# A transformer block on one core: the last unit in two tiles of 128 tokens, denominators from four key tiles, Q blocks moved

## The chip, the core and the metric

The kernel runs on one core of one Trainium2 chip. Five engines work side by side: TensorE (PE; its weight loads are shown as PEld) multiplies matrices, VectorE (DVE) and ScalarE (ACT) do elementwise work, GpSimd (POOL) small work, SyncE (SP) issues the transfers. SBUF is the memory that the engines work on, PSUM (8 banks of 128 x 512 fp32) takes the matmuls' results. The metric is device time in microseconds (us) of one launch.

## The reference

One pre-norm transformer block over 2048 tokens of width 1024, all bf16: LayerNorm, attention of 32 heads of 32, output projection and residual; LayerNorm, a feed-forward net of width 3584 with GELU (tanh form), residual.

```python
x = A_x
h = x + _A_ref(_layernorm(x, axis=-1), A_wqkv, A_wo)      # qkv, softmax(q k^T / sqrt(32)) v, wo
h2 = h + _B_ref(_layernorm(h, axis=-1), B_w1, B_b1, B_w2, B_b2)   # gelu(x w1 + b1) w2 + b2
```

The attention weights are 32 x 2048 x 2048 exponentials, and there is a plain softmax over the whole row, with no maximum taken off in the kernel.

## The kernel before

**Tiles.** Heads go in 8 groups `g` of four (4 x 32 = 128 partitions), queries in 8 blocks `qb` (also called units `u`) of 256 tokens. A *job* is one group and one query block. It has 8 *rounds*, each over 256 keys (two key tiles of 128): scores for four heads in one go (`Att.qk`, L756: 8 matmuls of 32 x 128, each head in its own quarter of the rows of the array, 256 queries as columns), two exponentials of 128 x 1024 on ScalarE into `PT` (L779), and P times V (`Job.pv`, L798: 8 matmuls, each head in its own quarter of the columns). The denominators are matmuls with a 32-column block of ones (`Job.den`, L828). To halve their number VectorE first adds the two key tiles of a round into `PS` (L820, three buffers), so a denominator of a round is four matmuls; the last round of a job goes straight from `PT` and takes eight. `Job.finish` (L842) transposes and inverts the denominators and writes the output of the job, transposed, to `OT`, which holds three query blocks (`u = qb % 3`).

**Background.** All that isn't attention (projections, Wo, LayerNorm, FFN) is cut into pieces that fill one of PSUM's banks 6 and 7 (`slot()`); a running job holds one of them for its output and denominators, banks 0 to 5 hold scores. `late_q` (L676) makes Q for a block of 512 tokens from a copy of the normalised x that was stored to DRAM (`x_scratch`), with the weights loaded again; `proj` (L635) makes it from SBUF, where `xnT` and the weights `Wall` lie until the FFN's buffers (`hch`, `gT`, the weight rings of `Rings`) are put over them. Either way Q goes to DRAM (`q_scratch`) and comes back a job at a time (`load_q`, L669). `wo` (L886) makes Wo and the residual of a unit into `hch`, `ln2` (L914) the LayerNorm and its transposes into `hnT`, `ffn1` (L925) the first FFN matrix in 14 blocks of 256 columns with bias on VectorE (L943) and a GELU of five VectorE operations and one tanh (`gelu`, L956), `ffn2` (L969) the second in two halves of 512 columns. W1 and Wo come through a ring of 4 blocks, W2 through one of 7.

**The end.** Unit 7 is worked when attention is over: `wo(7, True)` into banks 0 to 3 with the residual added by a matmul with the identity and drained by ScalarE, then `ffn1(7, True)` with ScalarE's own GELU from PSUM (L952), then both halves of `ffn2`. Its W1 goes into SBUF where K and V lay (`b_w1r`), its FFN1 output over `PT` (`gT7`).

**Order.** The code lists tasks with the buffers they read and write. `Graph.schedule` (L109) then simulates the engines with a cost for each task (`occ`), a latency behind it (`lat`) and 0.1 us for each change of array shape on TensorE, and so fixes one order for each engine, the DMA queue on SP too. `pick_pe` (L1144) chooses for TensorE: scores first, then the closing denominator of a job, P times V when enough rounds wait, else background in the order of listing. `merge_tiles` turns longer stretches of background from four 32-column matmuls into whole ones. On the chip each engine works its list in order and waits on semaphores. The listing from the first FFN unit on is (L1098 to L1123):

```python
    late_q(1, 1, [g for g in range(2, G) if g not in EXTRA])
    wo(0)
    ln2(0)
    late_q(2, 0, range(G))
    late_q(3, 1, range(G))
    ffn1(0)
    ...
    for u in range(6):
        wo(u + 1); ffn2(u, 0); ln2(u + 1); ffn2(u, 1); ffn1(u + 1)
        if u < 5:
            attention(u + 3, range(G))
```

(The loop's five calls stand on lines of their own in the file.) Attention thus runs two units and more ahead of the FFN, and the FFN of a unit can't begin before all eight jobs of that unit are finished.

Of the kernel before, what the change touches and what calls it, by code (L numbers as in the profile page):

```python
# [12 lines left out]
P = 128  # L13
# [47 lines left out]
class Graph:  # L61
# [47 lines left out]
    def schedule(self, pick_pe, pool, switch=0.1, dma_rate=280.0, dma_lat=2.1, dma_issue=0.06):  # L109
# [219 lines left out]
def build_kernel(nc, A_x, A_wqkv, A_wo, B_w1, B_b1, B_w2, B_b2, out):  # L329
# [22 lines left out]
    class Area:  # L352
        def __init__(self, start):
            self.cur = start
# [54 lines left out]
    B_OT = [B_OT_[G * i:G * i + G] for i in range(3)]  # L409
    xrb, B_xrb = sb(ot_lo, "xrb", [P, 8, D], BF, 8)  # L410
# [7 lines left out]
    xnT, B_xnTt = sb(ph0, "xnT", [P, 4, DC, 512], BF, 4, 4)  # L418
    k_hi = Area(B_KT[8 * (G - 2)].lo)
    Wall, B_W = [], []  # L420
    for k in range(6):
        h, b = sb(k_hi if k == 2 else ph0, "Wall%d" % k, [P, DC, 512], BF, 1, 4)
        Wall.append(h)
        B_W.append(b)
# [20 lines left out]
    gT7, B_gT7 = sb(Area(pt_lo), "gT7", [P, FC, 256], BF, FC // 2)  # L445
    gs, B_gs = [gT] * 7 + [gT7], [B_gT] * 7 + [B_gT7]
# [22 lines left out]
    att_area = Area(att_lo)  # L469
    w2_area = Area(att_lo)  # L470
    R2 = Rings((att_area, 14), (w2_area, 7), att_area, 2, "b_")
    assert att_area.cur <= att_hi
# [15 lines left out]
    def c_dve_ps(n):  # L488
        return (120 + n) / 960.0 + 0.02

    def c_dve(n, x=1):
        return (62 + n / x) / 960.0 + 0.085

    def c_act(n, ap_bias=False):
        return 0.073 + (0.093 if ap_bias else 0.0) + n / 1200.0

    def pe(fns, occ, reads=(), writes=(), kind="bg", mode="full", prio=0, after=()):
        return gr.add(E.PE, fns, occ, 0.16, reads, writes, prio, kind, mode, after)
# [45 lines left out]
    def act(fn, n, reads=(), writes=(), prio=0, ap_bias=False, kind="", after=()):  # L544
        return gr.add(E.Activation, fn, c_act(n, ap_bias), 0.14, reads, writes, prio, kind, after=after)

    def dve(fn, occ, reads=(), writes=(), prio=0):
        return gr.add(E.DVE, fn, occ, 0.08, reads, writes, prio)
# [25 lines left out]
    def layer_norm(tiles, prio, norm="dve", stats=None):  # L574
# [6 lines left out]
        for k, (x_ap, B_x, o_ap, B_o) in enumerate(tiles):  # L581
            for c in range(2):
                dve(lambda v, c=c, k=k, x_ap=x_ap: v.bn_stats(st_l[:, i + k, 6 * c:6 * c + 6], x_ap[:, 512 * c:512 * c + 512]),
                    0.68, reads=B_x if isinstance(B_x, list) else [B_x], writes=[B_stl[i + k]], prio=(prio or 1) if stats is None else stats)
# [11 lines left out]
        for k, (x_ap, B_x, o_ap, B_o) in enumerate(tiles):  # L596
            eng, cost = (dve, 0.58) if norm == "dve" else (pool, 3.8)
# [4 lines left out]
    def transposes(src_ap, B_src, bank, dst_ap, B_dst, evac, prio):  # L602
# [9 lines left out]
        else:  # L612
            t = dve(lambda v: v.tensor_copy(dst_ap, src()), 0.70, reads=[bb(bank)], writes=[B_dst])
# [17 lines left out]
    def tr_tile(tt, bank, evac, prio=0):  # L631
        tc, t4 = divmod(tt, 4)
        transposes(xb[:, tt % NXB, :], B_xb[tt % NXB], bank, xnT[:, tc, :, t4 * P:(t4 + 1) * P], B_xnTt[tc][t4], evac, prio)

    def proj(which, g, tc, bank, evac, direct=False):  # L635

        blk, c = divmod(which * D + g * P, 512)
        for dc in range(DC):
            mm(bank, Wall[blk][:, dc, c:c + P], xnT[:, tc, dc, :], dc == 0, dc == DC - 1,
# [55 lines left out]
    def proj_v(tt, q, bank, evac, after=()):  # L695
# [3 lines left out]
        for k in range(2):  # L699
            tc, t4 = divmod(tt + k, 4)  # L700
            for dc in range(DC):
                mm(bank, xnT[:, tc, dc, t4 * P:(t4 + 1) * P], Wall[blk][:, dc, c:c + 256], dc == 0, dc == DC - 1,
# [7 lines left out]
    def proj_v1(tt, g, n, bank, evac, c0=0):  # L710

        for k in range(n):
            tc, t4 = divmod(tt + k, 4)
            for dc in range(DC):
                mm(bank, xnT[:, tc, dc, t4 * P:(t4 + 1) * P], Wall[4][:, dc, P * g:P * g + P], dc == 0, dc == DC - 1,
# [12 lines left out]
    def proj_half(which, hc, bank, evac):  # L728
# [3 lines left out]
        for dc in range(DC):  # L732
            mm(bank, Wall[blk][:, dc, 0:P], xnT[:, tc, dc, 256 * h:256 * h + 256], dc == 0, dc == DC - 1,
# [13 lines left out]
    class Att:  # L747
# [8 lines left out]
        def qk(self, job, r):  # L756


            qb, g = job
            qs = q_slots[qb, g]  # L760
            us = [self.unit % self.n_units, (self.unit + 1) % self.n_units]
            self.unit += 2
            fns, banks = [], []
            for i in range(2):
                for h in range(4):
                    k0 = (2 * r + i) * P

                    def fn(p, i=i, h=h, k0=k0):
                        return p.matmul(psum[:, 2 * us[h // 2] + h % 2, 256 * i:256 * i + 256],  # L769
                                        KT[32 * h:32 * h + 32, g, k0:k0 + P], QT[32 * h:32 * h + 32, qs, :],  # L770
# [4 lines left out]
            pe(fns, 0.224, reads=[B_KT[8 * g + r], B_QT[qs]], writes=banks, kind="qk", mode="row")  # L775
# [476 lines left out]
```

## Time and profile before

| what | value |
|---|---|
| median of 3 runs | 1100.74 us (1100.32 to 1102.1) |
| span of the profiled execution | 1099.2 us |
| its own whole time | not on the page; the median is 1.54 us above its span |
| mean granted TensorE clock | 0.997 |
| busy PE, DVE, ACT | 1056.5, 757.2, 1019.8 us |
| first and last exponential begin | 16.4 and 1030.0 us |
| DMA traffic | 174.43 MB, mean 159 GB/s |

A row of instructions gives line, engine, operation, output<-input, shape and count; then busy time, the mean of one, and the idle time of the engine ahead of them with what ended it. Matmuls overlap: 0.27 us is the length of one, not the distance to the next. In an answer in order of time the first column is the start, the second the length, and brackets hold the idle time of the engine ahead of it.

### The profile page before, as it was taken

The page shows a single profiled execution, that of the slowest core. Times are in us where ns is not written, and L with a number is a line of the kernel's source. Part 1 is how long each engine was busy: PE and PEld are TensorE (multiplying, and loading weights), DVE is VectorE, ACT ScalarE, POOL GpSimd, SP SyncE. Part 2 cuts the span into 40 slices and gives each one's busy share as a digit, 9 for nine tenths or more (in the row PEclk, how much of TensorE's full clock was granted, in tenths as well). Part 3 has the DMA queues.
Part 4 walks back from the last instruction along what each step waited for, and adds up shares of the span by engine and source line. Part 5 has one row for each costly group of instructions (what it writes and reads, how often), then busy time and mean ns, then how long its engine had stood idle before and what let it go on. Part 6 is the DMA issues. An engine that isn't in the chain of part 4 may idle for free.

```text
span 1099.2 us, 42056 instructions
## 1 busy us (share of the span) xinstructions
PE 1056.5 (96%) x19177; PEld 613.8 (56%) x19226; DVE 757.2 (69%) x1444; ACT 1019.8 (93%) x1124; POOL 47.8 (4%) x110
## 2 busy tenths in 40 slices
PE   8899999998899999999999899999999999999998
PEld 6655555553345744664475456546744664565483
DVE  7746666665676886788588768876886787687501
ACT  3879999999999999999999999999999999999650
POOL 3200000000000001001000100010010000000100
PEclk9999999999899999999999999999999999999999
DMA  6820000048345654854576466448654747797370
GB/s 184 227 103 2 29 2 3 2 159 268 115 122 154 189 151 150 260 162 149 185 228 188 150 203 180 143 150 255 181 178 149 216 142 239 243 266 242 98 262 20
DMA packets 265506, 174.43 MB, mean 159 GB/s; under 512 B 26864, under 2 KB 260336, under 8 KB 264560
## 3 DMA queue, kind: packets, MB, share of 16 engines
q1 hardware_dynamic: 265328, 171.74, 51.2%
q8 instruction: 151, 2.47, 0.9%
q14 instruction: 27, 0.22, 0.1%
HBM read 161.23 MB, written 10.49 MB: 156 GB/s over the span
## 4 chain that ended last, share of the span: by engine, by line
ACT 79%; PE 19%; DVE 1%; issue 0%; DMA 0%; POOL 0%; POOLq 0%; DVEq 0%
ACT PT L779 75%; PE ps L540 6%; ACT uu L965 4%; PE ps L537 4%; PE ps L534 3%; PE ps L769 2%; PE ps L805 1%; PE ps L1007 1%; PE ps L834 1%; DMA a_w1r<-in_A_wo_dram 0%; ACT xnT L611 0%; PE ps L604 0%; DVE PS L820 0%; DVE OD L850 0%; DVE OD L857 0%
## 5 line engine op out<-in xcount | busy, mean ns | idle before, releaser
L779 ACT ACTIVATE PT<-ps 128x1024 bf16<-128x1024 f32 x1024 | 953.6, 1189 | 18.2 <-PE ps L769 18.0
L820 DVE TENSOR_TENSOR PS<-PT 128x1024 bf16<-128x1024 bf16 x434 | 287.5, 686 | 124.5 <-ACT PT L779 63.8
L769 PE MATMUL ps<-QT,KT 32*128 32x256 bf16 x4096 | 204.6, 273 | 13.5 <-ACT PT L779 10.2
L805 PE MATMUL ps<-PT,V 128*32 128x256 bf16 x4096 | 179.9, 273 | 1.5 <-ACT PT L779 1.1
L769 PEld LDWEIGHTS ps<-QT,KT 32*128 32x128 bf16 x4096 | 61.0, 92 | 174.1 <-ACT PT L779 165.3
L834 PE MATMUL ps<-PS,ones 128*32 128x256 bf16 x1736 | 121.7, 274 | 2.0 <-DVE PS L820 2.0
L805 PEld LDWEIGHTS ps<-PT,V 128*32 128x32 bf16 x4096 | 103.8, 97 | 30.0 <-issue 8.7
L537 PE MATMUL ps<-a_w2r,gT 128*128 128x512 bf16 x445 | 109.6, 380 | 4.9 <-issue 2.4
L537 PE MATMUL ps<-hnT,a_w1r 128*128 128x256 bf16 x903 | 111.2, 273 | 1.1 <-DVE rr L860 0.5
L534 PE MATMUL ps<-hnT,a_w1r 128*32 128x256 bf16 x2660 | 96.9, 274 | 2.4 <-DVE gT L943 1.2
L537 PEld LDWEIGHTS ps<-hnT,a_w1r 128*128 128x128 bf16 x903 | 82.7, 98 | 25.1 <-issue 14.8
L943 DVE TENSOR_TENSOR gT<-ps,b1f 128x512 bf16<-128x512 f32 x98 | 67.3, 687 | 27.7 <-PE ps L534 18.4
L534 PE MATMUL ps<-a_w2r,gT 128*32 128x512 bf16 x1140 | 81.6, 381 | 2.5 <-DVE OD L857 2.5
L534 PEld LDWEIGHTS ps<-hnT,a_w1r 128*32 128x32 bf16 x2660 | 66.2, 96 | 18.5 <-issue 14.0
L537 PEld LDWEIGHTS ps<-a_w2r,gT 128*128 128x128 bf16 x471 | 40.4, 98 | 55.3 <-issue 15.7
L989 DVE SCALAR_TENSOR_TENSOR hch<-ps,hch 128x512 bf16<-128x512 f32 x32 | 22.0, 689 | 64.0 <-PE ps L540 47.1
L834 PEld LDWEIGHTS ps<-PS,ones 128*32 128x32 bf16 x1736 | 45.9, 96 | 22.8 <-issue 8.7
L965 ACT ACTIVATE uu<-uu 128x1024 bf16<-128x1024 bf16 x49 | 58.0, 1206 | 0.0
L537 PE MATMUL ps<-xnT,Wall 128*128 128x512 bf16 (+1 forms) x213 | 47.7, 360 | 2.3 <-issue 1.1
L588 POOL CAST mvb<-mv 128x2 bf16<-128x2 f32 (+1 forms) x25 | 6.1, 242 | 990.0 <-DVE mv L585 987.2
L706 DVE CAST V<-ps 128x512 bf16<-128x512 f32 x32 | 22.1, 690 | 30.8 <-PE ps L537 15.8
L537 PE MATMUL ps<-Wall,xnT 128*128 128x256 bf16 x327 | 41.0, 273 | 0.0
(85 smaller groups left out, 1009.8 us busy)
## 6 DMA issues: line engine op xcount, KB each, us to landing
a_w2r<-in_B_w_dram SPq DMA_DIRECT2D x105, 512.0 KB, 5.6
a_w1r<-in_B_w_dram SPq DMA_DIRECT2D x98, 512.0 KB, 4.4
a_w1r<-in_A_wo_dram SPq DMA_DIRECT2D x32, 512.0 KB, 4.0
b_w1r<-in_B_w_dram SPq DMA_DIRECT2D x14, 512.0 KB, 5.8
a_w1r<-in_A_wqkv_dram SPq DMA_DIRECT2D x11, 512.0 KB, 4.3
xrb<-in_A_x_dram SPq DMA_DIRECT2D x16, 256.0 KB, 4.2
Wall<-in_A_wqkv_dram SPq DMA_DIRECT2D x16, 256.0 KB, 4.8
hch<-in_A_x_dram SPq DMA_DIRECT2D x16, 256.0 KB, 4.0
```

The costliest lines, as they stand in the source:

```text
L534: fns.append(lambda p, j=j: p.matmul(psum[32 * j:32 * j + 32, bi(bank), c0:c1], lhsT[:, 32 * j:32 * j + 32], rhs, start=start, stop=stop, ...
L537: t.whole = lambda p: p.matmul(psum[:, bi(bank), c0:c1], lhsT, rhs, start=start, stop=stop, skip_group_check=True)
L540: t = pe(lambda p: p.matmul(psum[:, bi(bank), c0:c1], lhsT, rhs, start=start, stop=stop), occ, reads=reads, writes=[bb(bank)], mode="full" ...
L706: t = dve(lambda v: v.tensor_copy(dst, psum[:, bi(bank), :].rearrange("p (t g c) -> p g t c", t=2, g=2)), c_dve_ps(512), reads=[bb(bank)], ...
L769: return p.matmul(psum[:, 2 * us[h // 2] + h % 2, 256 * i:256 * i + 256], KT[32 * h:32 * h + 32, g, k0:k0 + P], QT[32 * h:32 * h + 32, qs, :],
L779: act(lambda a, u=u, k=k: a.activation(PT[:, s, k, :, :], psum[:, 2 * u:2 * u + 2, :], ACT.Exp, bias=0.0, scale=SCALE), 1024, reads=[B_ps[ ...
L805: fns.append(lambda p, i=i, h=h: p.matmul(psum[32 * h:32 * h + 32, bi(bank), 0:256], V[:, g, 2 * r + i, 32 * h:32 * h + 32], PT[:, s, h // ...
L820: dve(lambda v: v.tensor_tensor(PS[:, n, :, :], pairs[:, :, 0:256], pairs[:, :, 256:512], ALU.add), c_dve(1024, 2), reads=[B_PT[2 * s], B_ ...
L834: fns.append(lambda p, h=h, rhs=rhs, i=i: p.matmul(psum[32 * h:32 * h + 32, bi(bank), 256:512], ones32[:, :], rhs, start=False, stop=last, ...
L943: t = dve(lambda v: v.tensor_tensor(g[:, fc:fc + 2, :], psum[:, bi(bank), :].rearrange("p (f c) -> p f c", f=2), b1f[:, fc:fc + 2].unsquee ...
L965: act(lambda a: a.activation(w, w, ACT.Tanh, bias=0.0, scale=KT2), 1024, reads=[B_uu[i]], writes=[B_uu[i]], prio=-1)
L989: drop(dve(lambda v, hs=hs, bank=bank, half=half: v.scalar_tensor_tensor(hch[:, hs, c], psum[:, bi(bank), :], half, hch[:, hs, c], ALU.mul ...
```

## The change

- **Denominators.** For rounds 0 and 1, 2 and 3, 4 and 5 of a job VectorE adds the two sums in `PS` once more, and one denominator of four matmuls stands for four key tiles. Round 6 keeps its own, round 7 still goes straight from `PT`.
- **Half jobs.** In query block 7 heads groups 6 and 7 are worked as half jobs of 128 queries: both groups for the first 128 tokens, then both for the second. A half job has 4 rounds of 512 keys; its matmuls have 128 columns, its exponentials the same 128 x 1024.
- **Unit 7 in two tiles.** Tile 0 (the first 128 tokens) goes through Wo, LayerNorm and FFN1 as background, with bias and GELU as in other units; tile 1 takes the former way of the end with 128 columns. FFN2 then runs tile by tile. W1 for the unit is loaded once, 12 blocks over K and V of groups 0 to 5 and two in the ring; two blocks of Wo are loaded again for tile 1 over K and V of group 6; the second half of W2 gets a place over `PT`. Both halves of FFN2 of unit 6 are listed ahead of Wo of unit 7.
- **Q blocks.** All Q projections of the second block of 512 tokens use `xnT` and `Wall` in SBUF. Its copy in DRAM isn't written any more. `late_q(2, 0)` is listed ahead of `wo(0)`. `xnT` is now one buffer for each 512 tokens, and the order of these and the weights in SBUF is another.
- **Places and costs.** Units 6 and 7 use places 0 and 2 of `OT` (`OS`). The planner's costs and latencies are other numbers; this changes the order of all engines, not what is computed.

```diff
-    def schedule(self, pick_pe, pool, switch=0.1, dma_rate=280.0, dma_lat=2.1, dma_issue=0.06):
+    def schedule(self, pick_pe, pool, switch=0.104, dma_rate=280.0, dma_lat=2.1, dma_issue=0.06):
...
+    OS = [0, 1, 2, 0, 1, 2, 0, 2]
...
-    xnT, B_xnTt = sb(ph0, "xnT", [P, 4, DC, 512], BF, 4, 4)
...
+    for kind, k in (("x", 1), ("W", 4), ("x", 0), ("x", 2), ("x", 3), ("W", 3), ("W", 5), ("W", 0), ("W", 1)):
+        h, b = sb(ph0, ("xnT%d" if kind == "x" else "Wall%d") % k, [P, DC, 512], BF, 1, 4)
...
+    gT7a, B_gT7a = sb(Area(ot_lo.start), "gT7a", [P, FC, P], BF, FC // 2)
+    w2b_area = Area(pt_lo)
+    w2b, B_w2b = sb(w2b_area, "w2b", [P, FC // 4, 4, 512], BF, FC // 4)
+    gT7b, B_gT7b = sb(w2b_area, "gT7b", [P, FC, P], BF, FC // 2)
...
+    W1B = [att_block(k, g, "w1b%d%d" % (g, k)) for g in range(6) for k in range(2)]
+    WOB = [att_block(k, 6, "wob%d" % k) for k in range(2)]
...
-        return (120 + n) / 960.0 + 0.02
+        return (120 + n) / 960.0 - 0.058
...
-        return (62 + n / x) / 960.0 + 0.085
+        return (62 + n / x) / 960.0
...
-        return gr.add(E.PE, fns, occ, 0.16, reads, writes, prio, kind, mode, after)
+        return gr.add(E.PE, fns, occ, 0.225 if isinstance(fns, list) and len(fns) > 1 else 0.2, reads, writes, prio, kind, mode, after)
...
-        return gr.add(E.DVE, fn, occ, 0.08, reads, writes, prio)
+        return gr.add(E.DVE, fn, occ, 0.135, reads, writes, prio)
...
+            kt = 512 // n
...
-            pe(fns, 0.224, reads=[B_KT[8 * g + r], B_QT[qs]], writes=banks, kind="qk", mode="row")
+            pe(fns, 0.224 if kt == 2 else 0.34, reads=B_KT[8 * g + kb * r:8 * g + kb * r + kb] + [B_QT[qs]], writes=banks, kind="qk", mode="row")
...
+    FOURS = (0, 2, 4)
...
-                self.sums.append((n, False))
+                if nq == 256 and r in FOURS:
+                    self.half = n
+                elif nq == 256 and r - 1 in FOURS:
+                    o = self.half
+                    dve(lambda v: v.tensor_tensor(PS[:, n, :, :], PS[:, n, :, :], PS[:, o, :, :], ALU.add), c_dve(1024, 2),
+                        reads=[B_PS[n], B_PS[o]], writes=[B_PS[n]], prio=-2)
+                    self.sums.append((n, False))
+                else:
+                    self.sums.append((n, False))
...
+    def ffn1_half(t, tail):
+        g, B_g = g7[t], B_g7[t]
+        for q in range(FC // 4):
+            bank = q % 6 if tail else slot()
+            for f in range(4):
+                w, B_w = w1_last[2 * q + f // 2]
+                for dc in range(DC):
+                    mm(bank, w[:, dc, (f % 2) * P:(f % 2) * P + P], hnT[:, dc, t * P:t * P + P], dc == 0, dc == DC - 1,
+                       [B_w, B_hnT[t]], not tail, (P * f, P * f + P))
...
-        if hc in (3, 5, 7):
+        if hc in (5, 7):
...
+    def attention_half(qb, gs, half):
+        for g in gs:
+            if half == 0:
+                load_q(qb, g)
+            job = Job(qb, g, slot(2), P * half, P)
+            for r in range(4):
+                attention_round(job, r)
+        attention_drain()
...
-    for g in range(2):
+    for g in range(G):
         if g not in EXTRA:
             proj(0, g, 1, slot(), "dve")
-    late_q(1, 1, [g for g in range(2, G) if g not in EXTRA])
+    late_q(2, 0, range(G))
     wo(0)
     ln2(0)
-    late_q(2, 0, range(G))
     late_q(3, 1, range(G))
...
-    for u in range(6):
+    for u in range(5):
...
-        if u < 5:
-            attention(u + 3, range(G))
-    attention_drain()
+        attention(u + 3, range(G) if u < 4 else range(6))
+    attention_half(7, (6, 7), 0)
+    attention_half(7, (6, 7), 1)
+    wo(6)
+    ffn2(5, 0)
+    ln2(6)
+    ffn2(5, 1)
+    ffn1(6)
+    load_w1_last()
     ffn2(6, 0)
-    wo(7, True)
-    ln2(7, True)
-    ffn2(6, 1, True, R1, (None, 5))
-    ffn1(7, True)
-    ffn2(7, 0, True, R1, (0, 1))
-    ffn2(7, 1, True, R2, (2, 3))
+    ffn2(6, 1)
+    wblocks = wo(7, (0,))
+    load_w1_rest()
+    ln2(7, (0,))
+    ffn1_half(0, False)
+    for k, (h, b) in enumerate(WOB):
+        dma(h[:, :, :], A_wo[:, 256 * k:256 * k + 256].rearrange("(dc p) c -> p dc c", p=P), P * DC * 512, writes=[b], prio=1)
+    wo(7, (1,), True, WOB + wblocks[2:])
+    ln2(7, (1,), True)
+    W20 = ffn2_weights(0)
+    ffn2_tile(7, 0, 0, W20, gT7a, B_gT7a, 0, 0.5, slot(), ())
+    ffn1_half(1, True)
+    W21 = ffn2_weights(1, True)
+    ffn2_tile(7, 1, 0, W21, gT7a, B_gT7a, 0, 0.5, slot(), ())
+    ffn2_tile(7, 0, 1, W20, gT7b, B_gT7b, 0, 1.0, 2, ())
+    ffn2_tile(7, 1, 1, W21, gT7b, B_gT7b, 0, 1.0, 3, ())
```

## The prediction

> **What bounds the kernel now.** I read the page first (busy shares, slices, chain, groups), then the stretches, then the order of instructions at the end.
>
> ```profile
> PE 1056.5 (96%) x19177; PEld 613.8 (56%) x19226; DVE 757.2 (69%) x1444; ACT 1019.8 (93%) x1124; POOL 47.8 (4%) x110
> ...
> ACT  3879999999999999999999999999999999999650
> ...
> ACT 79%; PE 19%; DVE 1%; issue 0%; DMA 0%; POOL 0%; POOLq 0%; DVEq 0%
> ...
> L779 ACT ACTIVATE PT<-ps 128x1024 bf16<-128x1024 f32 x1024 | 953.6, 1189 | 18.2 <-PE ps L769 18.0
> L820 DVE TENSOR_TENSOR PS<-PT 128x1024 bf16<-128x1024 bf16 x434 | 287.5, 686 | 124.5 <-ACT PT L779 63.8 <-PE ps L834 57.0
> ```
>
> ScalarE runs exponentials back to back from 71 us on (1024 of them in 953.6 us, 0.93 each), with 3.1 us of gaps until the last one. The chain is ScalarE up to there and TensorE behind it: three slices at the end in which ScalarE falls away. So two things set the time: when the last exponential ends, and how much TensorE work is left then.
>
> ```profile
> 250.00:260.00 10.00, 7.81 (x140) 3.36 (x140) 5.97 (x12) 10.00 (x12) 0.00 (x0) 1.00 0.80 249
> 270.00:280.00 10.00, 6.53 (x152) 2.80 (x140) 5.50 (x11) 10.00 (x12) 0.00 (x0) 0.88 0.68 215
> 280.00:290.00 10.00, 10.00 (x114) 3.88 (x114) 5.16 (x9) 8.46 (x10) 0.22 (x2) 0.78 0.01 3
> 550.00:660.00 110.00, 106.47 (x2040) 63.05 (x2045) 84.32 (x161) 110.00 (x121) 3.32 (x8) 1.00 0.64 192
> 880.00:990.00 110.00, 106.08 (x2188) 62.47 (x2191) 83.65 (x160) 109.93 (x121) 3.39 (x8) 1.00 0.74 224
> 1031.00:1099.00 68.00, 64.77 (x434) 40.29 (x439) 11.49 (x23) 19.43 (x37) 3.40 (x8) 1.00 0.38 126
> ```
>
> (Stretch, length, busy PE, PEld, DVE, ACT, POOL, granted clock, DMA share, GB/s.) In the middle ScalarE is full and TensorE nearly so; VectorE has a quarter free. Only around 250 to 285 has TensorE a hole, followed by a granted clock of 0.88 and 0.78.
>
> ```profile
> 1010.91 0.40 PE L769 MATMUL ps<-QT,KT 32*128 32x256 bf16 x8
> 1011.24 1.47 PE L537 MATMUL ps<-a_w2r,gT 128*128 128x512 bf16 x6
> ...
> 1027.97 0.28 PE L834 MATMUL ps<-PS,ones 128*32 128x256 bf16 x4
> 1028.08 0.39 PE L805 MATMUL ps<-PT,V 128*32 128x256 bf16 x8
> 1028.30 0.28 PE L834 MATMUL ps<-PS,ones 128*32 128x256 bf16 x4
> ```
>
> The start of the next row is what a row costs: a denominator of four matmuls 0.11 us (1027.97 to 1028.08), P times V of a round 0.22, scores of a round 0.33 with the change of array shape behind them, so about 0.114 for that change. Summing the streaming time of all matmuls that start in 440 to 660 gives 180 us of 220, 229 changes of shape at 0.114 give 26, and some 13.5 us are waits. By this count the waits are about 64 us between 110 and 1031. TensorE is full, not merely busy: what is taken from it counts, as long as other work is ready.
>
> ```profile
> 1030.02 1.07 ACT L779 ACTIVATE PT<-ps 128x1024 bf16<-128x1024 f32 x1
> 1040.36 0.62 PE L604 MATMUL ps<-ident,b_xb 128*128 128x128 bf16 x8
> 1040.82 4.70 PE L540 MATMUL ps<-a_w2r,gT 128*128 128x512 bf16 x20
> 1046.15 1.02 ACT L611 ACTIVATE hnT<-ps 128x1024 bf16<-128x1024 bf16 x1 [4.11 <-PE ps L604]
> 1047.25 3.00 PE L540 MATMUL ps<-hnT,b_w1r 128*128 128x256 bf16 x26
> 1071.92 12.03 PE L540 MATMUL ps<-a_w2r,gT 128*128 128x512 bf16 x54
> 1096.07 0.69 DVE L989 SCALAR_TENSOR_TENSOR hch<-ps,hch 128x512 bf16<-128x512 f32 x1 [5.35 <-PE ps L540]
> ```
>
> The last exponential ends at 1031.1; 68.1 us follow. TensorE does in them Wo of unit 7 (36 matmuls of 512 columns at 0.216: 7.8), 16 transposes (0.9), the rest of unit 6's second FFN2 half (31 x 0.216: 6.7), FFN1 (224 of 256 columns at 0.109: 24.4) and FFN2 (112 x 0.216: 24.2), and 3.1 us are the last add and store. That is 67.1 of the 68.1: the end is TensorE work without a hole.
>
> **The change part by part.**
>
> **1, denominators from four key tiles.** In 60 of the 62 jobs with summed pairs (two become half jobs) three of seven summed denominators go: 180 x 0.11 = 19.8 us less on TensorE, spread over the whole run. Each is replaced by an add of 128x1024 bf16 on VectorE, 0.609 from start to start (L820 back to back): 110 us more on VectorE. A 15 us job gets three, so 550 to 660 goes from 84.3 to about 97 of 110. The cover is the quarter of VectorE that is free; an eviction behind such an add comes 0.61 later, and TensorE then waits for its bank. Bounds: 0, and 110 us if all of it were exposed. I take 0 for the sum, since the adds are spread and their stretches stay under 0.9, and keep the rest as a rival.
>
> **2, Q blocks.** Three weight blocks, a block of x and the write of a copy of x go (3.7 MB in all); the five Q projections stay, from SBUF. What was waited for: TensorE's holes of 2.2 us (250 to 260, ahead of the first reloaded projection at 256.5) and 3.5 us (270 to 280, before Wo could have the last attention output), and the half clock behind the second, in which matmuls of 512 columns took 0.43 and not 0.216, some 2 us. The late Q block put ahead of Wo has 32 matmuls x 2 x 0.216 = 14 us for the second hole. Its weights and x are 3 MB, 12 us at 249 GB/s; late, they would open the hole again (bounds 0 and 8 us, I take 8 gained, since the ring they go to no longer lies on Q weights). Wo's loads and hch's are queued on SP behind them, but Wo has until 280 anyway; unit 0's LN2, POOL's work in it too, comes up to 14 us of TensorE later, ahead of nothing that ScalarE waits for. ScalarE's two gaps at 282 and 285 (1.5 us) should go with it: the end of the last exponential moves to 1029.6.
>
> **3, half jobs.** Two jobs of 8 rounds become four of 4, so 16 rounds have scores and P times V in four groups of 128 columns, not two of 256. A group costs between 0.055 (half of 0.11) and 0.11 (no gain). I take 0.08: 16 x 2 x (0.32 - 0.22) = 3.2, and denominators (ten groups a half job, 0.99 us a whole one) 4 x 0.8 - 2 x 0.99 = 1.2; together 4.4 us on TensorE (0.2 to 9.4). Per round that is some 1.2 us with denominators and shape changes, against 1.83 of ScalarE: hidden by the exponentials.
>
> **4, FFN1 of the last unit by 128 columns.** 448 matmuls instead of 224 of twice the width. Nearest row: the transposes, 8 of 128 columns in 0.46 us (1040.36 to 1040.82), each with its own weights, 0.057. The other end is 0.109. At 0.056, 12.5 us a tile, 0.6 in all. Tile 0 adds bias on VectorE and takes the tanh path; in column mode part of it costs 0.08, up to 2.7 us, if it runs among attention. Its 3.5 tanh (0.94 each) are on ScalarE behind the last exponential by step 5, else 3.3 us ahead of it.
>
> **5, what moves ahead of the last exponential.** The second half jobs of heads 6 and 7 are 16 exponentials, 14.7 us. So tile 0's last output is there about 12 us before the end of the last exponential (from the last exponential to OT the end took 2.7: 1031.1 to 1033.8). Wo of tile 0 starts with group 7 and takes 3.5 us of TensorE among rounds, 5 to 6 of time; LN2 from the residual to its transposes took 5.4 in the tail (1040.1 to 1045.5), and 0.7 for the eviction. FFN1 of tile 0 thus starts about when the last exponential ends. Behind it lie: FFN1 tile 0 12.5, Wo tile 1 (36 x 0.109) 3.9, transposes 0.5, FFN1 tile 1 12.5, FFN2 24.2, last add and store 3.1; 56.7 in all. LN2 of tile 1 (about 8 us) is covered by FFN2 of tile 0, 12.3 us; without that cover it would cost its 8. With the 1 us of small gaps of before, 57.7 against 68.1: 10.4 less. The new loads (unit 7's W1, 12 blocks = 6.3 MB into dead K and V from 29 us before the end, 25 us at 252 GB/s) just make it. The two blocks of W1 that go through the ring wait for Wo of tile 0, and the copies of Wo behind them on SP for the last P times V of head 6, some 7 us before the end of the exponentials; 1 MB, 4 us. The second half of W2 lies over P and can load only from the last P times V on (3.7 MB, 15 us); it is first read some 16 us later at the earliest, as filler, and needed 36 later.
>
> **6, planner's costs and places in SBUF.** The order of every engine is made anew. The waits of 64 us may shrink or grow; 0 for the sum, the ends are those of the rivals.
>
> **Sum.** By TensorE's work alone: -19.8 - 8 + 4.4 + 3.3 = -20.1, so 1079.1. But unit 6's Wo can't start before unit 6's attention ends (907), which ScalarE sets, and the work behind the last exponential stays 57.7 us. 1029.6 + 57.7 = 1087.3, the later of both. So 8 of TensorE's 20 us are slack ahead of unit 7. The profiled span is 1099.2; the page gives no other time for that execution, and the median of the three runs, 1100.74, is 1.54 above it. 1087.3 + 1.54 = 1088.8.
>
> **The rivals.**
>
> A, *VectorE gives it back* (slower). Evictions of FFN1 and Wo stand behind 180 more adds, and TensorE, with one spare bank, stops. For it: L820 already sat 57 us waiting for denominators and 64 for exponentials with the queue behind it, and the last GELU product of unit 6 came at 1014.1, 14 us after its last eviction, with TensorE idle 1.1 for it. Against: 13 us still free in 110. Price: an exposed add costs 0.61; above 13 of them (8 us) the end moves, at 33 of 180 (20.1 us) all is gone. At one in three, 37 us: 1099.2 - 20.1 + 37 = 1116, 1118 as a run.
>
> B, *128 columns do not halve a matmul*: with weight loads of 98 ns (L537's PEld rows) not covered, 448 x 42 ns = 18.8 us, nearly all in the tail. Against: the transposes' 57 ns. At a price of 81 ns it is 11.2: 1098.5, 1100 as a run, no change. The Trainium skill has that very figure, about 81 ns a matmul at N=128 in a stream of weight load and matmul ("TensorE: Matmul & The Clock Gate", Back-to-back issue gap); the transposes here speak against it, as they carry loads too.
>
> C, *the order gives more*: FFN1 of tile 0 gets ahead of the last exponential (the half jobs leave TensorE 0.6 us a round), up to 12.5 less; half of it or all, 1075 to 1082.
>
> D, *the change's end comes late*: W1 blocks or GELU of tile 0 hold the tail, or the second hole stays; 3 to 9 us: 1092 to 1098.
>
> **How the numbers follow.** Forecast (1084 to 1092) 0.52, C 0.18, D 0.10, A 0.13, B 0.07. Within 0.2% (2.2 us, what a measurement of this kernel can tell) falls B; faster is forecast, C and D: 0.80, same 0.07, slower 0.13. The range runs from C's middle, 1077, to the upper edge of B, 1102; the forecast's own is 1084 to 1092.
>
> **What would show it.** L834 (PS) from 1736 to some 1056 matmuls; a new PS<-PS group of 180 adds near 0.69; DVE near 860 us; no half clock near 280, and no xq read for Q block 1; the last exponential within 3 us of 1030; then 57 us of TensorE; hnT matmuls of 128 columns at 0.056. It is wrong if TensorE's waits on VectorE grow, if exponentials get new gaps, or if the matmuls of 128 columns cost 0.08 or more.

## The result, and the profile after

The changed kernel takes 1115.43 us (1114.67 to 1117.36, 4 runs) where the kernel before takes 1101.22: a ratio of 1.0125, 95% interval 1.011 to 1.014. It is slower by 1.25%, and the forecast of 1088.8 us and its range are missed. The profiled executions have spans of 1113.2 and 1099.2 us, 14.0 apart.

The page of the changed kernel: busy times, the slices of ScalarE and of the granted clock, the chain, and the groups that answer to those shown of before.

```profile
PE 1048.6 (94%) x18931; PEld 603.0 (54%) x18988; DVE 877.8 (79%) x1661; ACT 1017.6 (91%) x1125; POOL 51.1 (5%) x110
...
ACT  4889999999999999999999999999999999998331
PEclk9999999999999999999999999999999999998999
...
ACT 79%; PE 14%; DVE 4%; issue 1%; POOL 1%; DMA 0%; POOLq 0%; DVEq 0%
...
L793 ACT ACTIVATE PT<-ps 128x1024 bf16<-128x1024 f32 x1024 | 957.4, 1204 | 20.9 <-PE ps L782 20.6
L837 DVE TENSOR_TENSOR PS<-PT 128x1024 bf16<-128x1024 bf16 x432 | 294.4, 687 | 104.6 <-ACT PT L793 86.5
...
L843 DVE TENSOR_TENSOR PS<-PS 128x1024 bf16<-128x1024 bf16 x180 | 123.5, 686 | 3.7
...
L860 PE MATMUL ps<-PS,ones 128*32 128x256 bf16 (+1 forms) x1056 | 70.5, 270 | 3.4 <-issue 1.7
```

The work moved as the diff says: 1056 summed denominators, 180 new adds of 686 ns. VectorE is busy 120 us more, TensorE 8 us less. VectorE, 1% of the chain before, is now 4% of it. The exponentials are as many (1024, busy for 957.4 us, before 953.6), and the wait ahead of them for scores grew from 18.0 to 20.6 us.

The loss has two halves. The last exponential ends at 1038.0 and not at 1031.1 (6.9 us later), and behind it lie 75.2 us and not 68.1 (7.1 more). Of the 6.9 us, 2.4 are there when the last 32 exponentials, those of the half jobs, begin; 4.5 are lost among them. First the exponentials: ScalarE and TensorE in order of time, in the last rounds of the half jobs.

```profile
1010.83 11.11 ACT L793 ACTIVATE PT<-ps 128x1024 bf16<-128x1024 f32 x12
1023.79 1.94 ACT L793 ACTIVATE PT<-ps 128x1024 bf16<-128x1024 f32 x2 [1.85 <-PE ps L782]
1026.85 11.18 ACT L793 ACTIVATE PT<-ps 128x1024 bf16<-128x1024 f32 x12 [1.12 <-PE ps L782]
```

```profile
1020.37 0.22 PE L822 MATMUL ps<-PT,V 128*32 128x128 bf16 x1
1023.00 0.40 PE L822 MATMUL ps<-PT,V 128*32 128x128 bf16 x15 [2.42 <-issue]
1023.34 0.40 PE L782 MATMUL ps<-QT,KT 32*128 32x128 bf16 x16
1023.91 2.34 PE L548 MATMUL ps<-a_w2r,gT 128*128 128x512 bf16 x5 [0.17 <-issue]
1026.18 0.61 PE L782 MATMUL ps<-QT,KT 32*128 32x128 bf16 x16
...
1038.43 0.22 PE L860 MATMUL ps<-PT,ones 128*32 128x128 bf16 x1
1040.66 0.40 PE L860 MATMUL ps<-PT,ones 128*32 128x128 bf16 x15 [2.01 <-issue]
1041.39 7.46 PE L548 MATMUL ps<-a_w2r,gT 128*128 128x512 bf16 x27 [0.33 <-issue]
1048.69 3.62 PE L548 MATMUL ps<-a_w1r,OT 128*128 128x512 bf16 x16
```

TensorE stops for 2.42 us in the middle of a group of 16 matmuls, with no semaphore to wait for ("issue"; the last section tells what transfers show of it). Behind that its clock is halved: five matmuls of 512 columns take 2.34 us, where five took 1.25 at 1014.28. The next scores come late twice, and ScalarE has holes of 1.85 and 1.12 us. At 1038.65 the same happens again, 2.01 us and a half clock. From 72 us to its last exponential ScalarE has 11.4 us of gaps, before 3.3. Between 30 us and the last few us the clock was halved six times, each time for 3.4 us, and before once, for 6.8 us (at 278, which is gone).

Then the end. Unit 6's second FFN2 half (L548 from a_w2r at 1041.39) ends behind the last exponential, and Wo of tile 0 of unit 7 (L548 from a_w1r) comes only behind that. So all of unit 7 stands behind all of unit 6: its last FFN2 eviction is at 1048.9, and 64.3 us follow. In the kernel before, 1047.4 and 51.7. That eviction, before and after:

```profile
1047.45 0.69 DVE L989 SCALAR_TENSOR_TENSOR hch<-ps,hch 128x512 bf16<-128x512 f32 x1 [1.28 <-PE ps L540]
```

```profile
1048.89 0.69 DVE L1056 SCALAR_TENSOR_TENSOR hch<-ps,hch 128x512 bf16<-128x512 f32 x1 [6.51 <-PE ps L548]
```

One more table, of stretches: length, busy PE, PEld, DVE, ACT, POOL, clock, DMA share, GB/s. Before, then after:

```profile
940.00:1000.00 60.00, 58.21 (x1337) 38.81 (x1327) 45.75 (x87) 59.93 (x66) 0.00 (x0) 1.00 0.84 252
```

```profile
940.00:1000.00 60.00, 55.81 (x1216) 36.27 (x1210) 53.52 (x100) 58.57 (x64) 0.95 (x2) 0.97 0.84 251
1000.00:1030.00 30.00, 24.33 (x492) 11.81 (x497) 18.32 (x40) 25.85 (x29) 0.00 (x0) 0.89 0.55 169
```

In 960 to 1000, where most of FFN1 of unit 6 is evicted, VectorE is busy 38.26 of 40 us (33.72 before). The last GELU product of unit 6 ends 21.3 us after its last FFN1 eviction begins (14.9 before), and FFN2 waits for it.

### The profile page after: what moved, and what is told of

It is laid out like the page before. It is cut to its first block, busy times and chain, and to the rows that moved or that the text cites. A ratio compares the mean times of both kernels' runs of the same rounds, so it can differ in the third digit from the quotient of the medians.

```text
span 1113.2 us, 41816 instructions
## 1 busy us (share of the span) xinstructions
PE 1048.6 (94%) x18931; PEld 603.0 (54%) x18988; DVE 877.8 (79%) x1661; ACT 1017.6 (91%) x1125; POOL 51.1 (5%) x110
## 4 chain that ended last, share of the span: by engine, by line
ACT 79%; PE 14%; DVE 4%; issue 1%; POOL 1%; DMA 0%; POOLq 0%; DVEq 0%
ACT PT L793 74%; PE ps L548 5%; ACT uu L997 4%; PE ps L545 2%; PE ps L551 2%; PE ps L782 2%; PE ps L822 1%; PE ps L1079 1%; DVE PS L837 1%; PE ps L860 1%; ACT xnT L622 1%; DMA a_w1r<-in_A_wo_dram 0%; DVE st L594 0%; PE ps L615 0%; POOL denb L603 0%
## 5 line engine op out<-in xcount | busy, mean ns | idle before, releaser
L793 ACT ACTIVATE PT<-ps 128x1024 bf16<-128x1024 f32 x1024 | 957.4, 1204 | 20.9 <-PE ps L782 20.6
L837 DVE TENSOR_TENSOR PS<-PT 128x1024 bf16<-128x1024 bf16 x432 | 294.4, 687 | 104.6 <-ACT PT L793 86.5
L782 PE MATMUL ps<-QT,KT 32*128 32x256 bf16 (+1 forms) x4224 | 204.8, 271 | 12.4 <-ACT PT L793 7.9
L822 PE MATMUL ps<-PT,V 128*32 128x256 bf16 (+1 forms) x4224 | 171.0, 272 | 5.4 <-issue 2.4
L548 PE MATMUL ps<-a_w2r,gT 128*128 128x512 bf16 x473 | 121.5, 392 | 9.6 <-issue 3.4
L843 DVE TENSOR_TENSOR PS<-PS 128x1024 bf16<-128x1024 bf16 x180 | 123.5, 686 | 3.7
L548 PE MATMUL ps<-hnT,a_w1r 128*128 128x256 bf16 (+1 forms) x960 | 115.5, 271 | 1.3 <-DVE rr L888 0.5
L548 PEld LDWEIGHTS ps<-hnT,a_w1r 128*128 128x128 bf16 x960 | 87.0, 98 | 26.4 <-issue 14.8
L548 PEld LDWEIGHTS ps<-a_w2r,gT 128*128 128x128 bf16 x508 | 44.3, 100 | 65.6 <-issue 22.9
L997 ACT ACTIVATE uu<-uu 128x1024 bf16<-128x1024 bf16 (+1 forms) x53 | 64.0, 1227 | 16.2 <-DVE uu L996 16.2
L860 PE MATMUL ps<-PS,ones 128*32 128x256 bf16 (+1 forms) x1056 | 70.5, 270 | 3.4 <-issue 1.7
L548 PE MATMUL ps<-xnT,Wall 128*128 128x512 bf16 (+1 forms) x227 | 52.4, 365 | 2.7 <-DVE rr L888 1.2
L545 PE MATMUL ps<-xnT,Wall 128*32 128x512 bf16 (+1 forms) x736 | 45.5, 353 | 1.0 <-DVE OD L885 0.7
L548 PE MATMUL ps<-Wall,xnT 128*128 128x256 bf16 x328 | 41.1, 273 | 0.8 <-ACT xnT L622 0.8
```

Source lines behind the costliest of these rows:

```text
L545: fns.append(lambda p, j=j: p.matmul(psum[32 * j:32 * j + 32, bi(bank), c0:c1], lhsT[:, 32 * j:32 * j + 32], rhs, start=start, stop=stop, ...
L548: t.whole = lambda p: p.matmul(psum[:, bi(bank), c0:c1], lhsT, rhs, start=start, stop=stop, skip_group_check=True)
L782: return p.matmul(psum[:, 2 * us[h // 2] + h % 2, n * i:n * i + n], KT[32 * h:32 * h + 32, g, k0:k0 + P], QT[32 * h:32 * h + 32, qs, q0:q0 ...
L793: act(lambda a, u=u, k=k: a.activation(PT[:, s, k, :, :], psum[:, 2 * u:2 * u + 2, :], ACT.Exp, bias=0.0, scale=SCALE), 1024, reads=[B_ps[ ...
L822: fns.append(lambda p, i=i, h=h: p.matmul(psum[32 * h:32 * h + 32, bi(bank), 0:nq], V[:, g, kt * r + i, 32 * h:32 * h + 32], PT[:, s, h // ...
L837: dve(lambda v: v.tensor_tensor(PS[:, n, :, :], pairs[:, :, 0:256], pairs[:, :, 256:512], ALU.add), c_dve(1024, 2), reads=[B_PT[2 * s], B_ ...
```

## The experiments

Kernels that were measured together shared their runs of the kernel before, whose medians were 1101.44 to 1102.04 us. Ratios are to those, with 95% intervals. Spans and times within a run are of one profiled execution each.

### One part alone, one part undone

**Q blocks alone** in the kernel before, with its old costs: the places of xnT and Wall, and the order:

```
-        if hc in (3, 5, 7):
+        if hc in (5, 7):
...
-    for g in range(2):
+    for g in range(G):
...
-    late_q(1, 1, [g for g in range(2, G) if g not in EXTRA])
+    late_q(2, 0, range(G))
...
-    late_q(2, 0, range(G))
```

> The kernel before with the Q part alone (second Q block from SBUF, its copy not written, late Q block ahead of the first Wo, the other order of xnT and weights in SBUF). If the prediction's step 2 holds, the TensorE hole at 270 to 280 and the half clock behind it go and the last exponential ends 1.5 us earlier: 1098 to 1100 us. If the hole comes back elsewhere, or the gain is slack ahead of unit 6: 1101, no change.

1098.32 us, ratio 0.996 (0.9943 to 0.9977). The last exponential ends at 1028.5 instead of 1031.1, the end behind it is 68.2 us. **Planner's costs alone**, all the numbers that the diff changes in c_dve_ps, c_dve, c_act, the latencies and the switch:

```
-        return (120 + n) / 960.0 + 0.02
+        return (120 + n) / 960.0 - 0.058
...
```

> The kernel before with the planner's new costs and latencies alone; the work is the same, only the order of the engines differs. Theory H (half jobs and an empty background are to blame): within 3 us of 1101. Rival C (the new order is the cause): most of the 14 us shows here, 1108 or more.

1100.45 us, 0.9987 (0.9973 to 1.0): no measurable change. So neither of these parts lost the time.

**Denominators back to two key tiles** in the changed kernel:

```
-    FOURS = (0, 2, 4)
+    FOURS = ()
```

> The changed kernel with the denominators of two key tiles again (no second add). Rival V (VectorE's 180 adds make bias and GELU late, TensorE stands, its clock halves): back to 1103 or less. Theory H: the stall of 2 us inside P times V and the half clocks after 1000 stay, 1109 to 1114.

1106.9 us (1103.72 to 1110.59), 1.0045 (1.0027 to 1.0064). **Whole jobs** in place of the half jobs, with the two tiles and four key tiles kept:

```
-        attention(u + 3, range(G) if u < 4 else range(6))
-    attention_half(7, (6, 7), 0)
-    attention_half(7, (6, 7), 1)
+        attention(u + 3, range(G))
```

> The changed kernel with whole jobs for heads 6 and 7 of the last query block (256 queries); the unit is still worked in two tiles behind them. Theory H: the last exponential ends within 3 us of 1030 (1038 with half jobs), no stall of 2 us with no releaser on TensorE: 1102 to 1107 us, since the tail loses the stalls too. Rival V: no change, 1112 to 1117, or slower, as tile 0 comes still later.

1101.41 us, 0.9992 (0.9976 to 1.0008). Each of the two undone gives back most of the loss (8.5 and 14.0 us), so they must be crossed.

**Both undone**, whole jobs and FOURS = ():

> The changed kernel with neither half jobs nor the second adds; unit 7 in two tiles behind attention, Q part and costs as changed. If both causes add up (8.5 and 14 us apart): 1093 to 1097. If they are one cause (the same idle time of TensorE counted twice): 1099 to 1102.

1098.94 us, 0.9978 (0.9966 to 0.999). And the **former end of the kernel** (one tile of 256 tokens) with Q blocks and costs, first with two key tiles:

> The kernel before with Q part and costs, nothing else: the former end, whole jobs, two key tiles. If the two alone add (0.4% and 0.1%): 1096 to 1099. Against the run with the tiles in its place it prices the two-tile end with whole jobs: theory, the former end is 2 to 5 us quicker, since the tiles wait twice for LayerNorm and tile 0's GELU.

1097.65 us, 0.9965 (0.9953 to 0.9977), below both kernels; then with the second adds of the diff:

> As the run before with denominators of four key tiles in all blocks. Theory G: slower than without by 5 to 10 us (the GELU of unit 6 late), 1102 to 1108. If TensorE's time is what counts (the prediction's step 1): faster by up to 8, 1089 to 1096.

1100.48 us, 0.9994 (0.9983 to 1.0006). The medians side by side:

| end of the kernel | two key tiles | four key tiles |
|---|---|---|
| former, 256 tokens | 1097.65 | 1100.48 |
| two tiles, whole jobs | 1098.94 | 1101.41 |
| two tiles, half jobs | 1106.9 | 1115.43 |

Two tiles alone cost about 1 us, inside the intervals. Four key tiles cost 2.5 to 2.8 us where they should have gained, and 8.5 beside half jobs. Half jobs cost 8.0 us, and 14.0 beside four key tiles. Of the diff only the Q blocks gain.

### The half jobs

**P times V of the half jobs allowed from two waiting rounds on**, where the planner asks for six and otherwise lets them pile up:

```
+    def pv_start():
+        n = pv_next[0]
+        return 2 if n < len(pvs) and pvs[n] in half_pv else PV_START
...
-                if t.kind == "pv" and ready_rounds(now) < PV_START and qks[-1].done is None:
+                if t.kind == "pv" and ready_rounds(now) < pv_start() and qks[-1].done is None:
```

> The changed kernel; P times V of the half jobs may begin when 2 rounds wait, not 6, so that their matmuls no longer come in bursts of two jobs. Theory S (bursts of twice as many instructions outrun TensorE's instruction supply, each stall of 2 us or more halves the clock for 3.4 us): no stall over 1.5 us with releaser issue after 1000, 1104 to 1108 us. Rival K (half jobs hold the banks that the background needs): the spread holds them longer, 1113 to 1120.

1111.47 us, 1.0086 (1.0061 to 1.0111): 4 us back. The same with two key tiles, and with four key tiles in all but the last block:

> Half jobs spread, two key tiles in all blocks. Theory S: 1096 to 1100, 7 to 10 us under the same kernel with bursts (1106.9). If tile 0 now comes ahead of the last exponential, as the prediction's step 5 has it: 1088 to 1094, under both kernels. Rival K: 1105 or more.

> Half jobs spread as in the first run of this call, and four key tiles in query blocks 0 to 6 alone. Theory S: 1096 to 1101, as with whole jobs. If half jobs cost by their banks: 1103 or more.

1105.49 us, 1.0036 (1.0023 to 1.005), and 1106.87, 1.0043 (1.0027 to 1.0059): against 1106.9 and 1103.94 (below) without the spread there is no gain to speak of. The pile-up of rounds is not the main cause. A rival on record, that half jobs cost by holding the banks which the background needs, fits the last two times. So do the stalls, which stay: 1.83 to 2.56 us in the three kernels. The next run takes half jobs out and leaves their matmuls.

**Whole jobs whose matmuls are cut in two.** The kernel with both undone (1098.94 us), with the scores, P times V and denominators of block 7's groups 6 and 7 issued as twice as many matmuls of 128 columns. Jobs and banks stay, and in the traces VectorE, ScalarE and GpSimd have the same instructions in the same order; only the number of TensorE's instructions is that of half jobs.

```
+    def split(qb, g):
+        return 2 if qb == 7 and g >= 6 else 1
...
+                for c in range(split(qb, g)):
...
+                            return p.matmul(psum[:, 2 * us[h // 2] + h % 2, n * i + m * c:n * i + m * c + m],
```

> The run with whole jobs and two key tiles, the matmuls of its last two jobs (scores, P times V, denominators) each cut into two of 128 columns; jobs, banks, order and adds stay, the instructions of these rounds double. Theory S: stalls over 1.5 us after 1000, 1102 to 1108 us. Rival K: 1097 to 1101, as before the cut.

1107.3 us, 1.0049 (1.003 to 1.0068): 8.4 us slower than uncut, the whole price of half jobs with two key tiles, without a half job. TensorE uncut, then cut, around the same place:

```profile
1015.18 0.39 PE L822 MATMUL ps<-PT,V 128*32 128x256 bf16 x8
1015.40 0.82 PE L545 MATMUL ps<-a_w2r,gT 128*32 128x512 bf16 x12
...
1017.65 0.39 PE L545 MATMUL ps<-a_w2r,gT 128*32 128x512 bf16 x1 [0.56 <-issue]
```

```profile
1014.81 0.61 PE L545 MATMUL ps<-a_w2r,gT 128*32 128x512 bf16 x8
1015.25 0.28 PE L876 MATMUL ps<-PS,ones 128*32 128x128 bf16 x8
1015.36 0.40 PE L834 MATMUL ps<-PT,V 128*32 128x128 bf16 x16
1015.59 0.60 PE L545 MATMUL ps<-a_w2r,gT 128*32 128x512 bf16 x7
1019.48 0.61 PE L545 MATMUL ps<-a_w2r,gT 128*32 128x512 bf16 x5 [3.29 <-issue]
```

P times V of 16 matmuls takes 0.23 us to the next row, what 8 of 256 columns took (0.22): the narrower matmuls cost nothing in themselves. At 1016.2 TensorE then stands still for 3.29 us (0.56 in the uncut kernel); a half clock and ScalarE gaps of 3.72 and 1.03 us follow. Up to there this execution and the uncut one keep step (unit 6's first FFN2 half is evicted at 1002.9 and 1011.8 in both). Behind it the last exponential ends 4.5 us later, unit 6 5.8 us later, and the span is 7.0 us longer (1105.5 against 1098.5). So the number of TensorE's instructions in these rounds is enough for the price; the banks that half jobs hold are not needed for it. Not every such stall comes from cut matmuls: one of 2.11 us ends at 962.7, ahead of the first cut one (998.7), where the uncut kernel has 1.06.

### The four key tiles

**Second adds in all blocks but the last** (condition qb < 7 beside FOURS):

> The changed kernel with denominators of four key tiles in query blocks 0 to 6 alone; in block 7, beside which unit 6 is worked, two key tiles. Theory G (the added adds cost where unit 6's GELU must be ready for FFN2 that follows at once; in the blocks ahead TensorE's gain is slack): FFN2's first half of unit 6 is evicted some 11 us after FFN1's last block (22.7 in the changed kernel, 10.8 without any second adds) and the run takes 1104 to 1109. Rival E (the adds of all blocks delay alike, by half clocks and late banks): 1112 to 1115.

1103.94 us, 1.003 (1.0014 to 1.0045). With none it is 1106.9, with all 1115.43. So 162 of the 180 adds cost nothing that can be measured, and the 18 in block 7 come with 11.5 us. That is 0.64 each, about what one takes, but the next run shows that it is no price of an add.

**Two key tiles, with 18 second adds in block 7 into a tile that nothing reads**: the load on VectorE without any matmul depending on it.

> Half jobs with two key tiles in all blocks (1106.9 us); in query block 7 VectorE makes the second adds all the same, into a tile that nobody reads (18 adds, and the denominators stay as with two key tiles). If VectorE's load in the last block is what four key tiles cost there: half clocks near 945 and 1003 come back, GELU of unit 6 lags 20 us, 1110 to 1116. If it is the other order of TensorE's instructions: 1104 to 1109.

1108.49 us, 1.0058 (1.0041 to 1.0075), 1.6 us above 1106.9 and inside that kernel's scatter. In 960 to 1000 VectorE is as full as in the changed kernel (38.77 and 38.26 of 40 us), and the adds stand as early, with at most one operation between them and the pair sum. So neither VectorE's load nor the early place costs much by itself. **The second adds of block 7 at a late rank** in the changed kernel, behind the bank releases and evictions instead of ahead:

```
-                        reads=[B_PS[n], B_PS[o]], writes=[B_PS[n]], prio=-2)
+                        reads=[B_PS[n], B_PS[o]], writes=[B_PS[n]], prio=1 if self.qb == 7 else -2)
```

> The changed kernel; the second adds of block 7 are of low rank for VectorE (behind the release of a job's bank and the evictions, beside GELU). If the delay of banks and evictions is the cost: no half clock near 945 or 1003, 1105 to 1109. If it is the GELU lag or the sheer load: 1112 to 1117.

1105.96 us, 1.0036 (1.0023 to 1.0049), 9.5 us less with the same adds and the same matmuls. On VectorE the adds now come up to four operations later, no more. Taken with the run before, they cost only where they stand early and denominators wait for them. In this execution GELU of unit 6 is 15.8 us behind FFN1 and not 21.3, and the stalls of 2.42 and 2.01 us do not appear (the longest one is 0.90): the order on TensorE moved too, so how much of the 9.5 us is GELU's delay and how much is the stalls is not separated. A late GELU alone does not do it: with four key tiles it is 22.4 us behind with the former end and 23.7 with whole jobs, and these kernels take 1100.48 and 1101.41 us.

### Where tile 0's Wo stands

Open was whether tile 0 could have overlapped with the exponentials at all. **Wo, loads and LN2 of tile 0 numbered ahead of unit 6's second FFN2 half**, in three kernels:

```
-    ffn2(6, 1)
     wblocks = wo(7, (0,))
     load_w1_rest()
     ln2(7, (0,))
+    ffn2(6, 1)
```

> The changed kernel with one thing moved: Wo of tile 0 of the last unit, its loads and its LN2 are numbered ahead of unit 6's second FFN2 half instead of behind it. Theory 1 (the two tiles never overlapped because TensorE is behind by a fixed amount of work; the order of that work is worth only its holes): the holes of 1.06 and 0.79 us around the transposes of tile 0 go, the half clocks and stalls among the half jobs stay: 1111 to 1114 us. Theory 2 (step 5 of the prediction fell because tile 0's Wo was queued behind unit 6's FFN2; ahead of it, the tail shrinks towards the predicted 58 us): 1098 to 1106 us. Slower than the changed kernel would mean that the former place hid the loads of unit 7.

> The same move in the changed kernel with denominators from two key tiles (half jobs, 1106.9 us, where unit 6 is done early). Theory 1: holes only, 1104 to 1106 us. Theory 2: this is the case in which tile 0's Wo would overlap with the second half jobs as step 5 had it, 1093 to 1100 us.

> The same move in the kernel with whole jobs and two key tiles (1098.9 us). Here tile 0's Wo cannot begin before the last exponential's job, since a whole job gives both tiles their output at once. Theory 1: again only holes, 1097 to 1098.5 us. Theory 2: no earlier start to be had either, 1097 to 1099 us. The run tells whether this form, with the two tiles at the end, gets below the 1097.65 us of the former end with two key tiles.

In the changed kernel 1108.6 us, 1.006 (1.0047 to 1.0073), 6.8 less. With half jobs and two key tiles 1101.98, 1.0006 (0.9994 to 1.0018), 4.9 less. With whole jobs 1100.47, 0.9983 (0.9971 to 0.9995), no change from 0.9978. TensorE of the second of them:

```profile
1022.20 1.47 PE L548 MATMUL ps<-a_w1r,OT 128*128 128x512 bf16 x6
...
1032.22 0.23 PE L822 MATMUL ps<-PT,V 128*32 128x128 bf16 x2 [1.92 <-issue]
...
1035.46 5.13 PE L548 MATMUL ps<-a_w2r,gT 128*128 128x512 bf16 x23
1040.43 0.61 PE L615 MATMUL ps<-ident,a_xb 128*128 128x128 bf16 x8
1040.87 1.03 PE L548 MATMUL ps<-a_w2r,gT 128*128 128x512 bf16 x4
1041.82 10.89 PE L548 MATMUL ps<-hnT,w1b 128*128 128x128 bf16 x192
```

Here the overlap is what the prediction had: Wo of tile 0 at 1022, 6 us ahead of the last exponential's end (1028.2). FFN1 of tile 0 starts at 1041.82, right behind unit 6's last matmul. What follows that unit's last eviction is 57.8 us. Both theories were half right: the move gave more than its holes of 1.85 us, and yet no half-job kernel got below the whole-job ones.

The spans of the profiled executions are each the sum of two numbers, when unit 6's last FFN2 eviction comes and what is left behind it:

| kernel | last exponential ends | unit 6 ends | left | span |
|---|---|---|---|---|
| before | 1031.1 | 1047.4 | 51.7 | 1099.2 |
| former end, two key tiles | 1029.5 | 1044.3 | 52.0 | 1096.3 |
| two tiles, whole jobs, two key tiles | 1030.4 | 1034.5 | 64.1 | 1098.5 |
| half jobs, two key tiles | 1025.2 | 1037.6 | 64.3 | 1101.9 |
| half jobs, two key tiles, Wo ahead | 1028.2 | 1041.9 | 57.8 | 1099.8 |
| changed kernel, Wo ahead | 1034.4 | 1049.0 | 57.8 | 1106.8 |
| changed kernel | 1038.0 | 1048.9 | 64.3 | 1113.2 |

## Why the prediction was wrong, step by step

**What failed first is step 5**, which started FFN1 of tile 0 about when the last exponential ends and put 56.7 us behind that. The 56.7 us, 57.7 with its small gaps, were right (57.8 with Wo ahead), but they lie behind the end of unit 6, and the step never asked when unit 6 ends. An estimate could have been made from the trace of before: behind the last output of unit 6 (906.8) TensorE still had Wo (6.9 us), 92 of the 112 FFN2 matmuls of unit 5 (19.9), 16 transposes (0.9), FFN1 (24.4) and FFN2 of unit 6 (24.2), 76.3 us. FFN1 of unit 6 had 13 of its 14 banks evicted in 41.2 us (958.6 to 999.8), 22.7 us of matmuls, so the background gets 0.55 of the time. 76.3 at that rate needs some 138 us, and from 906.8 to 1031.1 there are 124.3. Of the 19.8 us that step 1 takes off TensorE, only 18 x 0.11 = 2.0 lie behind 906.8. So by this estimate unit 6 is not done when the exponentials are, and there is no room for FFN1 of tile 0; before, it was done 16 us later, and in no kernel less than 3.8 us later. The prediction saw the evidence, the 31 FFN2 matmuls of unit 6 in the tail of before, and left them out of its new tail. They are not free TensorE time: they filled the tail's holes, and in the changed kernel unit 7 waited for them.

**Step 1** mis-sized the cover. Matmuls and adds were counted exactly (1056, 180 at 686 ns). But the stretch 550 to 660 was not the one that decides: in 960 to 1000 VectorE was at 0.96. The zero holds for blocks 0 to 6 and fails in block 7, where 18 adds come with 11.5 us beside half jobs. A full VectorE is not the whole reason, since 18 adds that nothing waits for cost 1.6 us at 0.97; which wait makes up the rest stays open. The 19.8 us of TensorE brought nothing measurable in any pair; with the former end they cost 2.8 us.

**Step 3** was too dear per group and blind to what groups do together. A group of four matmuls of 128 columns cost 0.055 us, its lower bound (16 matmuls in 0.22 to 0.23 us). "Hidden by the exponentials" failed: half jobs cost 8.0 us with two key tiles, and the cut matmuls alone 8.4, beside TensorE stalls of 2 to 3.3 us of which before shows no like (its longest of this kind is 1.21 us).

**Step 2** was right in direction and mechanism: no half clock near 280 in the kernel with the Q part alone, the last exponential 2.6 us earlier in one execution each (1.5 were taken), 0.4% in time. In the changed kernel a stall of 1.66 us at 275 of the same "issue" kind stands near that place, without a half clock.

**Step 4** held: 192 of the 224 matmuls of tile 0's FFN1 take 10.89 us, 57 ns each, 187 of tile 1's take 10.60. Rival B is out. The 81 ns a matmul at N=128 of the Trainium skill ("TensorE: Matmul & The Clock Gate", Back-to-back issue gap) is not what this kernel shows, with a weight load to every matmul.

**Step 6** held: the costs alone are within 0.13%, an interval that reaches 1.0.

**The rivals.** A gave 1116 to 1118 and is nearest in time, but by a third of all adds exposed over the whole run; in fact the 162 in blocks 0 to 6 cost nothing measurable, and the 18 in block 7 come with 11.5 us only beside half jobs (with whole jobs all 186 together cost 2.5). C's overlap came about only when Wo was moved ahead, and was then worth 4.9 to 6.8 us, not the 12.5 that it hoped for. D named what would hold the tail, and GELU is among it, though of unit 6 and not of tile 0; none of its prices reached 14 us. Under "what would show it" five marks came true or nearly (1056 matmuls, 180 adds, VectorE 878 for 860, no half clock near 280, 128 columns at 0.057), and the two that mattered did not: the last exponential within 3 us of 1030 (1038.0), and then 57 us (75.2). Its sign of being wrong, new gaps between the exponentials, appeared (11.4 us for 3.3).

## What to carry to other kernels

Before a late unit is split so that its first half may start early, add up what the engine still owes to the unit ahead, divide by the share of time it gets, and compare that with the time left. Work that is cut into smaller instructions of the same total length is not the same work: the cut alone cost 8.4 us here, so give it a run of its own. Whether an added operation is hidden can't be read from its engine's mean, nor from one full stretch: undo it in that stretch alone, and once keep it with nothing that waits for it.

## What the runs showed of the hardware

**Stalls tied to a place in TensorE's instruction stream.** Among half jobs or cut matmuls TensorE stops for 1.8 to 3.3 us with no semaphore to wait for. Counting recorded matmuls and weight loads from the start, the stall of 2.42 us in the changed kernel and that of 1.87 us in the one with Wo ahead stand at the same number, 35817; those of 2.81 and 1.92 us in the two kernels with half jobs and two key tiles both at 38131. There are eleven of over 1.8 us in these rounds, in eight kernels, and all stand between 229 and 247 modulo 256. Each run has 144 to 156 transfers of 16384 bytes on the queue that the profile calls "instruction"; the changed kernel's line is

```profile
q8 instruction: 149, 2.44, 0.8%
```

That is one for every 254 to 256 recorded matmuls and weight loads, in every kernel. When these transfers begin tells what the stalls wait for. Behind 100 us the 19 traces hold 50 TensorE stalls of 0.9 us or more to which the profile gives no releaser, and each of the 50 ends 2.2 to 2.9 us after such a transfer begins. Of the 92 as long that have a releaser 9 do, no more than by chance (0.11 of the time lies so). So by their timing TensorE waits there for its next instructions. No run changed their loading, and why some of these transfers come too late stays open. The rate alone does not decide: the densest 4 us hold 284 instructions at most without half or cut jobs and 340 to 400 with most of them, yet with P times V spread they hold 288 to 306, and stalls of up to 2.56 us remain. Kernels without half or cut jobs have such stalls too, elsewhere and up to 1.93 us.

**A half clock after short idling.** The granted clock fell to half for 3.4 us after 1.7 to 2.8 us of TensorE idle within the 6.8 us ahead, in pieces of 0.1 to 2.4 us (the six of the changed kernel). As much did not always do it: with half jobs, two key tiles and Wo ahead, 2.2 us of idle in the 6.8 up to 1035.5 brought no half clock. The Trainium skill ("TensorE: Matmul & The Clock Gate", What's actually happening) gives the same length, a free-running window of 3413 ns, but puts the fall after at least one idle window; here far less than a whole window of idling was enough.

**Scatter.** The kernel before stays within 1.8 us in its 4 runs beside the changed kernel, but spreads over 6.2 and 7.0 us in longer series (27 and 23 runs); the one with half jobs and two key tiles spreads over 6.9 us (10 runs). A trace is one execution out of such a spread: that of half jobs with two key tiles is the fastest of its ten (1103.72), that of whole jobs with four key tiles the slowest (1105.93). Times read from single traces, the table of spans included, are good to a few us.
